# Two 64-row tiles for the remainder products of a column DFT, inside a stream of full-height matmuls

## The chip, the cores and the metric

The kernel runs on one core of one Trainium2 chip. The metric is the device time of one execution in microseconds, median of several.

## The reference, cut to what matters

```python
x  = A_x                                  # 1 x 2048 x 640, bf16
xn = layernorm(x)
X  = rfft2(xn) * (w_r + 1j * w_i)         # over 2048 rows and 640 columns
y  = irfft2(X)                            # bf16
h  = (xn @ w_gate) * (xn @ w_up)          # 640 -> 1536
return x + y + h @ w_down
```

The DFTs are done as matmuls. The step concerned is the DFT over the 640 columns. Symmetry folds 640 columns to 160, and 160 is 128 + 32: each of four groups g (even and odd output columns, cosine and sine) is one product over 128 rows plus a remainder over 32 rows. The four remainders together fill another 128 rows.

## The kernel before: the parts that matter

The remainder table puts group g on rows 32 g to 32 g + 31, and its columns in one of two halves of 320. So the first half (groups 0, 1) has only zeros below row 63, the second half (groups 2, 3) only zeros above row 64:

```python
fd = np.zeros((128, 4 * 160 + 640))
for g in range(4):
    fd[:, g * 160:(g + 1) * 160] = full[g][0:128]                                  # main
    fd[g * 32:(g + 1) * 32, 640 + g * 160:640 + (g + 1) * 160] = full[g][128:160]  # remainder
```

There are 16 D steps, t = 0 to 15. Each has two remainder products of 320 columns (line 887 of the kernel) and four main products of 160 columns (line 891), in two PSUM banks:

```python
def em_d(c, t=t):
    bk = bank_of(c.t)
    for h in range(2):
        c.e.matmul(ps[:, bk + h, 0:320], v_uq[:, 4, t, :], v_fd[:, 640 + 320 * h: 960 + 320 * h],
                   start=True, stop=False)                                  # L887
        for g in (2 * h, 2 * h + 1):
            o = (g % 2) * 160
            ins = c.e.matmul(ps[:, bk + h, o:o + 160], v_uq[:, g, t, :],
                             v_fd[:, g * 160:(g + 1) * 160],
                             start=False, stop=(g % 2 == 1))                # L891
    return ins
td = T("D_%d" % t, "pe", 2 * _d_mm(320) + 4 * _d_mm(160), em_d, ..., prio=pq, bank="pair", cls="a")
```

`T` records a task. A planner in the kernel's own Python orders all tasks on all engines by estimated durations, gives PSUM banks and sets the semaphore waits; the order is fixed when the program is built. Other lines that appear below: L844 gate and up products, L912 to L915 the next complex DFT step (C), L945 and L962 the inverse of it, L985 and L989 the inverse column DFT, L1030 the down product, L926 VectorE's filter multiply, L859 VectorE's product of gate and up, L677 the PSUM eviction (on ScalarE here).

Of the kernel before, what the change touches and what calls it, by code (L numbers as in the profile page):

```python
# [538 lines left out]
def _build(nc, A_x, A_w_r, A_w_i, B_w_gate, B_w_up, B_w_down, out, opts=None):  # L539
# [3 lines left out]
    with es:  # L543
# [56 lines left out]
        ps = es.enter_context(nc.psum_tensor("ps", [128, 8, 512], _F32))  # L600
# [3 lines left out]
        def V(name):  # L604
            off, sz = lay[name]
            return arena[:, off: off + sz]
# [5 lines left out]
        v_uq = V("U").rearrange("p (j t n) -> p j t n", j=5, t=16)  # L612
# [8 lines left out]
        v_fd = V("FD")  # L621
# [40 lines left out]
        def bank_of(t):  # L662
            return t.units[1]
# [207 lines left out]
        for t in range(16):  # L871
# [11 lines left out]
            def em_d(c, t=t):  # L883
                bk = bank_of(c.t)
                ins = None
                for h in range(2):
                    c.e.matmul(ps[:, bk + h, 0:320], v_uq[:, 4, t, :], v_fd[:, 640 + 320 * h: 960 + 320 * h],  # L887
                               start=True, stop=False)
                    for g in (2 * h, 2 * h + 1):
                        o = (g % 2) * 160  # L890
                        ins = c.e.matmul(ps[:, bk + h, o:o + 160], v_uq[:, g, t, :], v_fd[:, g * 160:(g + 1) * 160],  # L891
                                         start=False, stop=(g % 2 == 1))
                return ins
            td = T("D_%d" % t, "pe", 2 * _d_mm(320) + 4 * _d_mm(160), em_d, reads=[(b_u, None), (b_fd, None)],
                   prio=pq, bank="pair", cls="a")

# [231 lines left out]
```

## Time and profile before

| what | before | where it is read |
|---|---|---|
| device time | 223.86 us (223.76 to 224.03) | median of 4 runs |
| span of the profiled run | 221.8 us | head of the page |

That PE is the bound while the D steps run (85 to 119 us) is read from its waits, and the prediction below shows the lines. It misses one stall, which the table of PE's waits doesn't list because the record of the product ahead covers all but 10 ns of it. Two lines of the trace before show it:

```profile
88.80 0.30 PE L891 MATMUL ps<-arena 128*128 128x160 bf16 x2
89.11 0.99 PEld L844 LDWEIGHTS ps<-arena 128*128 128x128 bf16 x10 [0.21 <-DVE arena L926]
```

The second L891 starts at 88.87, and L844 would follow 69 ns later; it starts 243 ns later, so PE stands for 174 ns, for VectorE's filter multiply by the second line. It is the only stall of more than 20 ns in the D steps' stretch.

### The profile page before, as it was taken

What the parts mean: (1) busy time and instruction counts of PE and PEld (TensorE: products, weight loads), DVE (VectorE), ACT (ScalarE), POOL (GpSimd) and SP (SyncE); (2) the same over time, 40 slices, a digit from 0 to 9 for tenths busy, and PEclk for the clock granted to TensorE, in tenths of its full rate; (3) what the DMA queues carried; (4) which work ended last, traced back from release to release, by engine and by line L of the source; (5) the groups of instructions that cost most, each with busy time, mean ns of one, the idle gap of its engine ahead of it and who ended that gap; (6) DMA issues with size and microseconds to landing.
All of it is one profiled execution on the core that took longest, in us unless ns stands there. A gap on an engine that the chain in (4) does not pass through costs nothing.

```text
span 221.8 us, 5449 instructions
## 1 busy us (share of the span) xinstructions
PE 216.7 (98%) x2204; PEld 184.3 (83%) x2204; DVE 162.2 (73%) x481; ACT 112.0 (50%) x225; POOL 0.2 (0%) x4
## 2 busy tenths in 40 slices
PE   8999999999999999999999999999999999999995
PEld 8988999999999998888888898888867777777773
DVE  3779999999999994999999958998994222222321
ACT  2576888677777777777777566556520000000000
POOL 0000000000000000000000000000000000000000
DMA  7999995000000000232232029200002332323211
GB/s 197 303 345 392 413 371 92 3 4 0 0 3 0 4 0 3 46 65 62 63 67 55 7 85 317 77 0 3 0 15 78 102 98 79 106 86 106 77 44 44
DMA packets 22184, 21.16 MB, mean 95 GB/s; under 512 B 2192, under 2 KB 21008, under 8 KB 21904
## 3 DMA queue, kind: packets, MB, share of 16 engines
q1 hardware_dynamic: 20048, 19.74, 29.5%
q10 hardware_dynamic: 2112, 1.08, 1.9%
q8 instruction: 17, 0.28, 0.5%
q14 instruction: 7, 0.06, 0.1%
HBM read 18.19 MB, written 2.62 MB: 94 GB/s over the span
## 4 chain that ended last, share of the span: by engine, by line
PE 87%; DMA 4%; DVE 3%; SPq 3%; issue 1%; ACT 0%
PE ps L844 43%; PE ps L1030 23%; DMA arena<-in_A_x_dram 4%; PE ps L945 3%; SPq L671 3%; PE ps L807 2%; PE ps L891 2%; PE ps L887 2%; PE ps L1032 2%; PE ps L985 2%; PE ps L989 2%; PE ps L764 2%; PE ps L962 2%; PE ps L913 1%; PE ps L914 1%; PE ps L912 1%
## 5 line engine op out<-in xcount | busy, mean ns | idle before, releaser
L677 ACT ACTIVATE arena<-ps 128x512 bf16<-128x512 f32 (+5 forms) x214 | 109.3, 543 | 47.0 <-PE ps L844 37.7
L844 PE MATMUL ps<-arena 128*128 128x256 bf16 (+1 forms) x1200 | 115.5, 251 | 0.6 <-ACT arena L677 0.5
L844 PEld LDWEIGHTS ps<-arena 128*128 128x128 bf16 x1200 | 96.1, 98 | 9.1 <-issue 0.7
L1030 PE MATMUL ps<-arena 128*128 128x320 bf16 x384 | 56.6, 299 | 0.0
L1030 PEld LDWEIGHTS ps<-arena 128*128 128x128 bf16 x384 | 37.5, 98 | 14.5
L1039 DVE TENSOR_TENSOR arena<-ps,arena 128x320 bf16<-128x320 f32 x32 | 15.7, 491 | 37.2 <-PE ps L1032 37.2
L859 DVE TENSOR_TENSOR arena<-arena 128x256 bf16<-128x256 bf16 (+1 forms) x120 | 30.9, 258 | 11.9 <-ACT arena L677 9.6
L926 DVE TENSOR_TENSOR arena<-ps,arena 128x644 f32<-128x644 f32 x32 | 24.9, 819 | 1.3 <-PE ps L915 1.3
L723 DVE BATCH_NORM_STATS2 arena<-arena 128x6 f32<-128x320 bf16 x16 | 7.8, 485 | 4.5 <-DMA arena<-in_A_x_dram 4.5
L796 DVE TENSOR_TENSOR arena<-arena 128x256 bf16<-128x256 f32 (+1 forms) x32 | 10.2, 318 | 0.0
L797 DVE TENSOR_TENSOR arena<-arena 128x256 bf16<-128x256 f32 (+1 forms) x32 | 10.2, 317 | 0.0
L985 PE MATMUL ps<-arena 66*128 66x320 bf16 x32 | 9.3, 301 | 0.6 <-DVE arena L1013 0.6
L945 PE MATMUL ps<-arena 128*128 128x256 bf16 x64 | 9.6, 273 | 0.0
L1032 PE MATMUL ps<-arena 128*128 128x320 bf16 x32 | 9.6, 299 | 0.0
L989 PE MATMUL ps<-arena 128*128 128x160 bf16 x64 | 9.3, 231 | 0.0
L891 PE MATMUL ps<-arena 128*128 128x160 bf16 x64 | 9.1, 233 | 0.0
L887 PE MATMUL ps<-arena 128*128 128x320 bf16 x32 | 9.1, 299 | 0.0
L1004 DVE TENSOR_TENSOR arena<-ps,arena 128x320 f32<-128x320 f32 x16 | 7.8, 485 | 0.3
L935 DVE TENSOR_TENSOR arena<-arena 128x322 bf16<-128x322 f32 x16 | 7.8, 487 | 0.1
L1012 DVE TENSOR_TENSOR arena<-arena 128x320 bf16<-128x320 f32 x16 | 7.7, 484 | 0.1
L936 DVE TENSOR_TENSOR arena<-arena 128x322 bf16<-128x322 f32 x16 | 7.8, 486 | 0.0
L786 DVE TENSOR_TENSOR arena<-arena 128x320 f32<-128x320 bf16 x16 | 7.7, 483 | 0.0
(45 smaller groups left out, 157.9 us busy)
## 6 DMA issues: line engine op xcount, KB each, us to landing
arena<-in_A_x_dram SPq DMA_DIRECT2D x20, 160.0 KB, 2.3
out_dram<-arena SPq DMA_DIRECT2D x32, 80.0 KB, 1.6
arena<-c_ti SPq DMA_DIRECT2D x1, 2048.0 KB, 18.1
arena<-in_B_w_down_dram SPq DMA_DIRECT2D x1, 1920.0 KB, 9.2
arena<-c_tf SPq DMA_DIRECT2D x4, 384.0 KB, 11.6
arena<-in_A_w_r_dram SPq DMA_DIRECT2D x32, 40.1 KB, 2.2
arena<-in_A_w_i_dram SPq DMA_DIRECT2D x32, 40.1 KB, 2.3
arena<-in_B_w_gate_dram SPq DMA_DIRECT2D x4, 320.0 KB, 7.7
```

Source lines behind the costliest of these rows:

```text
L677: return c.e.activation(dst, src, _ACTF.Copy)
L844: ins = c.e.matmul(ps[:, bk, w * n:(w + 1) * n], v_gw[:, w, j, ft, :], v_xt[:, j, rows], start=(j == 0), stop=(j == 4))
L859: return c.e.tensor_tensor(v_ht[:, ft, rows], v_gbf[:, rr, 0:n], v_gbf[:, rr, n:2 * n], _OP.mult)
L887: c.e.matmul(ps[:, bk + h, 0:320], v_uq[:, 4, t, :], v_fd[:, 640 + 320 * h: 960 + 320 * h], start=True, stop=False)
L891: ins = c.e.matmul(ps[:, bk + h, o:o + 160], v_uq[:, g, t, :], v_fd[:, g * 160:(g + 1) * 160], start=False, stop=(g % 2 == 1))
L926: ins = c.e.tensor_tensor(v_p[:, r2, w, :, :].rearrange("p c (m e) -> p c e m", e=2), x4, wv, _OP.mult)
L945: ins = c.e.matmul(ps[:, bk, lt * 256:(lt + 1) * 256], v_y[:, r2, cc, lt:256:2], v_ti[:, t, cc, :], start=(cc == 0), stop=(cc == 1))
L985: c.e.matmul(ps[:, bk + h, 0:320], v_z2[0:66, 2, h, a, :], v_g[0:66, 640 + 320 * h: 960 + 320 * h], start=True, stop=False)
L989: ins = c.e.matmul(ps[:, bk + h, e * 160:(e + 1) * 160], v_z2[:, e, h, a, :], v_g[:, g * 160:(g + 1) * 160], start=False, stop=(e == 1))
L1030: c.e.matmul(ps[:, bk, 0:320], v_ht[:, ft, a * 128:(a + 1) * 128], v_wd[:, ft, sl3], start=(ft == 0), stop=False)
L1032: return c.e.matmul(ps[:, bk, 0:320], v_sm[:, 2, :], v_v[:, a, sl3], start=False, stop=True)
L1039: return c.e.tensor_tensor(v_out[:, a % 2, sl3], ps[:, bk, 0:320], v_xr[:, xs, sl3], _OP.add)
```

## The change

The intent is to run the two half-empty remainder products at the same time, each as a 64-row tile of the array, and so to save one streaming slot of 320 columns in every D step.

```diff
                 for h in range(2):
-                    c.e.matmul(ps[:, bk + h, 0:320], v_uq[:, 4, t, :], v_fd[:, 640 + 320 * h: 960 + 320 * h],
-                               start=True, stop=False)
-                    for g in (2 * h, 2 * h + 1):
-                        o = (g % 2) * 160
-                        ins = c.e.matmul(ps[:, bk + h, o:o + 160], v_uq[:, g, t, :], v_fd[:, g * 160:(g + 1) * 160],
-                                         start=False, stop=(g % 2 == 1))
+                    c.e.matmul(ps[:, bk + h, 0:320], v_uq[64 * h:64 * h + 64, 4, t, :],
+                               v_fd[64 * h:64 * h + 64, 640 + 320 * h:960 + 320 * h], start=True, stop=False)
+                for g in range(4):
+                    o = (g % 2) * 160
+                    ins = c.e.matmul(ps[:, bk + g // 2, o:o + 160], v_uq[:, g, t, :], v_fd[:, g * 160:(g + 1) * 160],
+                                     start=False, stop=(g % 2 == 1))
                 return ins
```

In the built program the remainder products are tiles of 64 x 128 at array rows 0 and 64, and all other products keep the mode of 128 x 128.

## The prediction

> **What bounds the kernel now.** I read the busy row first, then the chain that ended last, then the table of who waited for whom, and last the order of instructions in time over one turn of the loop that is changed. The page:
>
> ```profile
> PE 216.7 (98%) x2204; PEld 184.3 (83%) x2204; DVE 162.2 (73%) x481; ACT 112.0 (50%) x225; POOL 0.2 (0%) x4
> PE 87%; DMA 4%; DVE 3%; SPq 3%; issue 1%; ACT 0%
> L891 PE MATMUL ps<-arena 128*128 128x160 bf16 x64 | 9.1, 233 | 0.0
> L887 PE MATMUL ps<-arena 128*128 128x320 bf16 x32 | 9.1, 299 | 0.0
> ```
>
> The reader is to see three things. PE is busy for 216.7 of 221.8 us and is 87% of the chain that set the end. The two lines that the change touches, L887 (the remainder product, 32 times) and L891 (the four main products of each D step, 64 times), have no idle time before them. And the 299 ns of one L887 is not its price: 32 of them are "9.1 us busy" and 64 of L891 another 9.1, but matmuls overlap, so a price is the distance from one start to the next. That is in the matmuls of one D step in order of time (columns: start us, length us, engine, line, operation, count):
>
> ```profile
> 104.34 0.38 PE L962 MATMUL ps<-arena 128*66 128x256 bf16 x2
> 104.56 0.30 PE L887 MATMUL ps<-arena 128*128 128x320 bf16 x1
> 104.69 0.30 PE L891 MATMUL ps<-arena 128*128 128x160 bf16 x2
> 104.83 0.30 PE L887 MATMUL ps<-arena 128*128 128x320 bf16 x1
> 104.96 0.30 PE L891 MATMUL ps<-arena 128*128 128x160 bf16 x2
> 105.10 1.26 PE L844 MATMUL ps<-arena 128*128 128x256 bf16 x10
> ```
>
> A D step runs from 104.56 to 105.10: 0.54 us for 2 x 320 + 4 x 160 = 1280 columns, 0.422 ns a column, so 135 ns for one L887. The start-to-start distance (104.56 to 104.69) says the same. The other 299 - 135 = 164 ns of its record lie under the next matmul. There are 16 D steps, from 85.10 to about 119.4 us.
>
> Whether time taken from PE there reaches the end is a question of who waits. PE itself waited, in the whole execution:
>
> ```profile
> PE ps L704 <- DVE arena L711: 1.0, 1, 1.0
> PE ps L985 <- DVE arena L1013: 0.6, 2, 0.5
> PE ps L844 <- ACT arena L677: 0.5, 1, 0.5
> PE ps L764 <- DVE arena L729: 0.2, 1, 0.2
> ```
>
> None of these is inside the D stretch. The stretch itself, by engine (window, length, then busy us of PE, PEld, DVE, ACT, POOL, granted clock, DMA share, GB/s):
>
> ```profile
> 96.00:108.00 12.00, 12.00 (x113) 10.24 (x112) 11.40 (x23) 9.57 (x19) 0.00 (x0) 1.00 0.30 63
> 108.00:121.00 13.00, 13.00 (x122) 11.24 (x120) 11.89 (x23) 9.75 (x18) 0.00 (x0) 1.00 0.28 61
> ```
>
> PE has no gap at all, while VectorE has 1.7 us of idle in 25. One turn takes 2.84 us (D steps at 101.71, 104.56, 107.40). VectorE's order in time shows where its slack sits: once a turn it stands 0.27 us waiting for a ScalarE eviction.
>
> ```profile
> 104.18 0.29 DVE L859 TENSOR_TENSOR arena<-arena 128x256 bf16<-128x256 bf16 x1 [0.27 <-ACT arena L677]
> 107.02 0.29 DVE L859 TENSOR_TENSOR arena<-arena 128x256 bf16<-128x256 bf16 x1 [0.27 <-ACT arena L677]
> ```
>
> So PE bounds this stage with 0.27 us a turn to spare before VectorE would. The queue that loads the filter rows is third: four issues a turn, about 0.64 us each (pairs take 1.24 with a small gap), some 2.55 of 2.84 us.
>
> **What the Trainium skill says.** (1) "TensorE: Matmul & The Clock Gate", Part 3: operands on different row groups of the array run at once, starting about 4 ns apart, so a pack of two should cost little more than one matmul. Nothing in the trace before shows this; it has no row-tiled product. (2) "TensorEngine Tiling (Array Packing)", Key Properties: "Changing tiling mode (not just tile) drains the TensorE". It gives no time for the drain, and again the trace before has none: every matmul, the 66-row L985 too, is built for the full 128 x 128 array. (3) "TensorE: Matmul & The Clock Gate", Part 2, says that the fill and drain of successive matmuls overlap, that the next weights are loaded while a matmul streams, and splits the latency of an isolated matmul into about 60 cycles of issue, 128 of array drain and 31 of others. The trace agrees on the overlap: matmuls 135 ns apart with records of 299 ns, and weight loads of 98 ns that begin before the preceding products are done.
>
> **The change part by part.** Products, results and work of all other engines stay the same. The remainder table is block-shaped: the first half of its columns has non-zero rows 0 to 63 only, the second half 64 to 127 only, so half heights lose nothing and numbers stay as they were.
> - Removed: one streaming slot of 320 columns a D step, since the two remainder products now run side by side in two 64-row tiles and write two different banks. 16 x 135 ns = **2.16 us** if the overlap is complete. All lies on PE's gapless path.
> - Moved: the second remainder product goes ahead of all four main products. The order of instructions on PE is otherwise unchanged: the planner is still told two full durations, so no step moves against another, and the number of matmuls and weight loads stays 2204.
> - Added: two changes of tiling mode a D step, full to 64-row and back, as each pair stands between full-height products even where two D steps follow each other. I counted 32 in the built program; before there are none. Each may put a drain on the path that before was overlapped.
>
> With d the exposed time of one change, the net is 32 d - 2.16 us, and the change breaks even at **d = 68 ns**. What d may be, from numbers at hand:
> - nothing (mode travels with the instruction): 223.87 - 2.16 = 221.7 us.
> - array drain alone: 128 cycles at 2.4 GHz is 53 ns, an estimate from the page under (3): 32 x 0.053 = 1.7, net -0.5, so 223.4 us.
> - the tail of the record, 164 ns, exposed: 5.25 - 2.16 = +3.1, so 227.0 us.
> - that tail and then a weight load that could not be pulled ahead, 164 + 98 = 262 ns: 8.4 - 2.16 = +6.2, so 230.1 us.
>
> **The rivals.**
> A: overlap without a price, 221.7 us. For it: PE is the bound, the saving of 0.135 us a turn fits VectorE's 0.27 us and the load queue's 0.29 us, so it would travel to the end whole; after 121 us PE has only the 0.6 us wait at L985, which shifts along. Against: the page's sentence on the drain.
> B: the drains take back the gain or more, 223.4 to 230 us. For it: the sentence, 32 changes against 16 savings, and the fact that PE has no waits under which a drain could hide; every nanosecond is on the path. I hold this likelier than A, with d in the middle, because a drain has to wait for the last product's results and then cannot have its next weights early.
> C: VectorE or the load queue becomes the bound and caps the gain. For it: 95% and about 90% busy in the stretch. Against: the slacks just named are twice the saving. Worth at most some tenths: it would make 222.0 to 222.5 of A.
> D: the two tiles don't overlap, as both stream from the same buffer. Then nothing is saved and the drains come on top: 225.6 (d = 53) to 229 (d = 164). Little in the profile speaks for or against.
>
> **Range and chances.** I give A (with C) 0.25, a drain of 50 to 110 ns 0.3, 110 to 200 ns 0.25 and more 0.2. The middle of this lies at d near 90 ns: 32 x 0.09 - 2.16 = +0.7, so **224.5 us**. Eight in ten: 221.6 to 229.0. Faster by over 2% (below 219.4) would need twice the whole saving: 0.01. Slower by over 2% (above 228.35) needs d above 208 ns, or no overlap with d above 140: 0.18. Within 2%: 0.81.
>
> **What would show each step.** In the order of instructions in time, the two remainder products (now 64 rows) should start a few ns apart; 135 ns apart is D. From the last product before the pair to the pair, and from the pair to the first main product, the start distances should exceed those before by d each; none is A. A D step should take 0.54 - 0.135 + 2 d. VectorE's idle of 0.27 us a turn should fall to 0.13 (A), or grow by the added time (B). The table of waits should show no new wait of PE; one on VectorE or on a filter-row load is C. The prediction is wrong if d is far from 90 ns, or if a weight load for a half-height tile costs more than the 98 ns of today.

## More of the kernel before

One more view is needed to read the result, the weight loads (PEld) of one D step before (start us, length us, then engine, line, operation, count):

```profile
104.20 0.25 PEld L962 LDWEIGHTS ps<-arena 128*66 128x66 bf16 x2
104.45 0.10 PEld L887 LDWEIGHTS ps<-arena 128*128 128x128 bf16 x1
```

The product L887 itself starts at 104.56. Its weights begin to load at 104.45, 0.11 us earlier, while the second L962 product still streams.

## The result, and the profile after

| | before | after |
|---|---|---|
| device time, us | 223.86 (223.76 to 224.03), 4 runs | 225.01 (224.53 to 225.07), 4 runs |
| ratio | | 1.0046, 95% interval 1.0029 to 1.0063 |
| span of the profiled run, us | 221.8 | 223.1 |
| one turn with a D step, us | 2.84 | 2.92 |

A ratio is the mean time of one kernel's fast runs over that of the other's of the same rounds, so it is not quite the ratio of the medians. The change is 0.5% slower: within 2%, but clear of noise.

The page after, busy row and chain:

```profile
PE 217.9 (98%) x2204; PEld 181.6 (81%) x2204; DVE 162.3 (73%) x481; ACT 112.3 (50%) x225; POOL 0.2 (0%) x4
PE 87%; DMA 4%; DVE 3%; SPq 3%; issue 1%; ACT 0%
```

PE is still the bound, with the same number of instructions. The two groups of the D step after, by shape (busy us, mean ns, then idle before):

```profile
L891 PE MATMUL ps<-arena 128*128 128x160 bf16 x64 | 7.2, 235 | 0.0
L887 PE MATMUL ps<-arena 64*128 64x320 bf16 x32 | 5.0, 307 | 0.0
```

L887 fell from 9.1 to 5.0 us busy and L891 from 9.1 to 7.2, and neither has any idle before it: by the groups alone one would think that 6 us were won. The busy time of a group counts overlapping records once, so it falls when two products overlap, and the tail of a record (307 ns for 135 ns of streaming) covers the gap behind it. The gap shows only in the starts. The matmuls of one D step after:

```profile
105.11 0.38 PE L962 MATMUL ps<-arena 128*66 128x256 bf16 x2
105.42 0.31 PE L887 MATMUL ps<-arena 64*128 64x320 bf16 x2
105.66 0.45 PE L891 MATMUL ps<-arena 128*128 128x160 bf16 x4
105.95 1.25 PE L844 MATMUL ps<-arena 128*128 128x256 bf16 x10
```

From L962 to L844 it is now 0.84 us; before it was 0.76 (104.34 to 105.10). Both remainder products lie in one record pair of 0.31 us, so they do run together. But L962 to L887 grew from 0.22 to 0.31 us, and the pair is followed by its first main product only 0.24 us later, where one product of 320 columns takes 0.14. The weight loads of the same step:

```profile
104.97 0.25 PEld L962 LDWEIGHTS ps<-arena 128*66 128x66 bf16 x2
105.42 0.10 PEld L887 LDWEIGHTS ps<-arena 64*128 64x128 bf16 x2 [0.20 <-DVE arena L859]
105.66 0.25 PEld L891 LDWEIGHTS ps<-arena 128*128 128x128 bf16 x4
```

The weights no longer load early: load and product now start together, at 105.42 and again at 105.66. The bracket names a VectorE instruction as the releaser, but the table of waits of the matmuls has no such row (that of the weight loads has: L887 on L859, 1.6 us in 8 of 32 loads):

```profile
PE ps L704 <- DVE arena L711: 1.0, 1, 1.0
PE ps L844 <- ACT arena L677: 0.7, 1, 0.7
PE ps L985 <- DVE arena L1013: 0.7, 2, 0.5
```

The releaser is inferred from the last semaphore event; the start distances below show the same gap in every D step, also in those whose loads have no bracket. The run e1 below has the same order of instructions at full height, and no such gap. The time went into gaps that no view calls a wait. VectorE, in its order of time, only stands longer for the eviction that PE now feeds later:

```profile
104.95 0.29 DVE L859 TENSOR_TENSOR arena<-arena 128x256 bf16<-128x256 bf16 x1 [0.35 <-ACT arena L677]
107.87 0.29 DVE L859 TENSOR_TENSOR arena<-arena 128x256 bf16<-128x256 bf16 x1 [0.35 <-ACT arena L677]
```

It was 0.27 us, and the turn grew by the same 0.08 us.

The trace keeps starts to the nanosecond. Medians of the distance from one start to the next over all D steps, worked out from the matmul records:

```
from -> to                              before   after
L962 (256 columns) -> first L887          109     205     +96
first L887 -> second L887                   -       3.5
last L887 (320 columns) -> L891           136     239     +103
first L891 after the pair -> next L891     69      80     +11
other L891 -> L891                         69      69
```

Other products ahead of a pair give the same: L844 109 to 205.5, L915 (322 columns) 135.5 to 230.5, L891 69 to 165. The sum for one D step: 96 + 103 + 11 + 3.5 is 213.5 ns lost, 136 ns saved, net 77.5 ns; times 16 is 1.24 us, against 1.15 us between the medians.

The spans differ by 1.24 us too, but in part by chance. From the product ahead of the first D step to the one behind the last, the trace before takes 34.34 us and the trace after 35.42: 1.08 us more. The missing 0.15 us is the stall at 88.87, which shrank from 174 to 21 ns. Another 0.15 us of the spans' difference lies ahead of the first D step, where the wait of L844 for an eviction (0.5 us listed before, 0.7 after) differs as much without any tiles (0.8 us in e1).

### The profile page after: what moved, and what is told of

It reads as the page before. It is cut to its first block, busy times and chain, and to the rows that moved or that the text cites. A ratio compares the mean times of both kernels' runs of the same rounds, so it can differ in the third digit from the quotient of the medians.

```text
span 223.1 us, 5449 instructions
## 1 busy us (share of the span) xinstructions
PE 217.9 (98%) x2204; PEld 181.6 (81%) x2204; DVE 162.3 (73%) x481; ACT 112.3 (50%) x225; POOL 0.2 (0%) x4
## 3 DMA queue, kind: packets, MB, share of 16 engines
q10 hardware_dynamic: 2112, 1.08, 1.8%
## 4 chain that ended last, share of the span: by engine, by line
PE 87%; DMA 4%; DVE 3%; SPq 3%; issue 1%; ACT 0%
PE ps L844 43%; PE ps L1030 23%; DMA arena<-in_A_x_dram 4%; PE ps L945 3%; SPq L671 3%; PE ps L891 3%; PE ps L807 2%; PE ps L1032 2%; PE ps L887 2%; PE ps L985 2%; PE ps L989 2%; PE ps L764 2%; PE ps L962 2%; PE ps L913 1%; PE ps L914 1%; PE ps L915 1%
## 5 line engine op out<-in xcount | busy, mean ns | idle before, releaser
L677 ACT ACTIVATE arena<-ps 128x512 bf16<-128x512 f32 (+5 forms) x214 | 109.6, 543 | 47.8 <-PE ps L844 37.4
L844 PE MATMUL ps<-arena 128*128 128x256 bf16 (+1 forms) x1200 | 115.5, 251 | 0.7 <-ACT arena L677 0.7
L844 PEld LDWEIGHTS ps<-arena 128*128 128x128 bf16 x1200 | 96.0, 98 | 9.2 <-issue 0.9
L1030 PE MATMUL ps<-arena 128*128 128x320 bf16 x384 | 56.6, 299 | 0.0
L859 DVE TENSOR_TENSOR arena<-arena 128x256 bf16<-128x256 bf16 (+1 forms) x120 | 31.1, 259 | 12.4 <-ACT arena L677 10.0
L926 DVE TENSOR_TENSOR arena<-ps,arena 128x644 f32<-128x644 f32 x32 | 25.0, 823 | 1.5 <-PE ps L915 1.5
L985 PE MATMUL ps<-arena 66*128 66x320 bf16 x32 | 9.3, 301 | 0.7 <-DVE arena L1013 0.7
L945 PE MATMUL ps<-arena 128*128 128x256 bf16 x64 | 9.6, 273 | 0.0
L1032 PE MATMUL ps<-arena 128*128 128x320 bf16 x32 | 9.6, 300 | 0.0
L989 PE MATMUL ps<-arena 128*128 128x160 bf16 x64 | 9.3, 232 | 0.0
L1012 DVE TENSOR_TENSOR arena<-arena 128x320 bf16<-128x320 f32 x16 | 7.8, 487 | 0.1
L1013 DVE TENSOR_TENSOR arena<-arena 128x320 bf16<-128x320 f32 x16 | 7.8, 486 | 0.0
L786 DVE TENSOR_TENSOR arena<-arena 128x320 f32<-128x320 bf16 x16 | 7.8, 485 | 0.0
L785 DVE TENSOR_TENSOR arena<-arena 128x320 f32<-128x320 bf16 x16 | 7.8, 485 | 0.0
```

The costliest lines, as they stand in the source:

```text
L677: return c.e.activation(dst, src, _ACTF.Copy)
L844: ins = c.e.matmul(ps[:, bk, w * n:(w + 1) * n], v_gw[:, w, j, ft, :], v_xt[:, j, rows], start=(j == 0), stop=(j == 4))
L859: return c.e.tensor_tensor(v_ht[:, ft, rows], v_gbf[:, rr, 0:n], v_gbf[:, rr, n:2 * n], _OP.mult)
L926: ins = c.e.tensor_tensor(v_p[:, r2, w, :, :].rearrange("p c (m e) -> p c e m", e=2), x4, wv, _OP.mult)
L945: ins = c.e.matmul(ps[:, bk, lt * 256:(lt + 1) * 256], v_y[:, r2, cc, lt:256:2], v_ti[:, t, cc, :], start=(cc == 0), stop=(cc == 1))
L985: c.e.matmul(ps[:, bk + h, 0:320], v_z2[0:66, 2, h, a, :], v_g[0:66, 640 + 320 * h: 960 + 320 * h], start=True, stop=False)
```

## The experiments

My theory: each change between full-height and 64-row mode exposes about 0.1 us on PE, because the array must be empty before the next weights may load; the two tiles overlap fully; nothing else changed. Rivals: (R1) the order of the products costs time; (R2) the pair doesn't overlap fully and changes are cheap; (R3) any product of fewer rows than its neighbours stalls, whatever the mode; (R4) the gap is a late weight load and not the array. All experiments change only the D step; those of one table row are against the kernel before on the same chip.

| run | change of the D step | mode changes | overlapped slots | this, us | before, us | ratio (95%) |
|---|---|---|---|---|---|---|
| e1_full_reordered | order only | 0 | 0 | 223.92 | 223.89 | 0.9997 (0.9979 to 1.0015) |
| e2_one_half_tiled | one product tiled | 32 | 0 | 227.32 | 223.89 | 1.0151 (1.0133 to 1.0169) |
| e3_four_changes | both tiled, apart | 64 | 0 | 230.35 | 223.89 | 1.0288 (1.0269 to 1.0308) |
| e4_same_tile | both on one tile | 32 | 0 | 227.07 | 223.89 | 1.0142 (1.0115 to 1.017) |
| e5_66_rows | one product of 66 rows | 0 | 0 | 223.93 | 223.84 | 1.0000 (0.9986 to 1.0015) |
| v2_quad | two D steps in one, tiled | 16 | 16 | 224.31 | 223.84 | 1.0015 (1.0003 to 1.0028) |
| v3_quad_full | the same at full height | 0 | 0 | 224.82 | 223.84 | 1.0036 (1.0022 to 1.005) |
| v4_local_batches | tiled only where D steps adjoin | 6 | 7 | 224.29 | 223.97 | 1.0009 (0.9995 to 1.0022) |
| e6_96_columns | narrower tile weights | 32 | 16 | 225.23 | 223.97 | 1.0052 (1.0038 to 1.0065) |

The record marks all nine as correct. That includes e4 and e6, whose remainder products are wrong, so the mark says nothing about the remainder products of the others.

### e1_full_reordered: the order alone

```diff
-                    c.e.matmul(ps[:, bk + h, 0:320], v_uq[64 * h:64 * h + 64, 4, t, :],
-                               v_fd[64 * h:64 * h + 64, 640 + 320 * h:960 + 320 * h], start=True, stop=False)
+                    c.e.matmul(ps[:, bk + h, 0:320], v_uq[:, 4, t, :], v_fd[:, 640 + 320 * h:960 + 320 * h],
+                               start=True, stop=False)
```

> Both remainder products first, as in the changed kernel, but at full height: the order alone, no tiling. Drain theory (each change of tiling mode exposes about 100 ns on PE: (225.01 - 223.86 + 2.16) / 32 = 0.103 us): as the kernel before, 223.9 us, D step 0.54 us. Rival (the order itself, writing the second bank early, delays PE or an eviction): 224.5 to 225.

223.92 us against 223.89. The start distances are those of before (109, 136, 136, 69 ns). R1 falls.

### e2_one_half_tiled: two changes, no overlap

```diff
-                for h in range(2):
-                    c.e.matmul(ps[:, bk + h, 0:320], v_uq[64 * h:64 * h + 64, 4, t, :],
-                               v_fd[64 * h:64 * h + 64, 640 + 320 * h:960 + 320 * h], start=True, stop=False)
+                for h, r in ((0, slice(0, 64)), (1, slice(0, 128))):
+                    c.e.matmul(ps[:, bk + h, 0:320], v_uq[r, 4, t, :], v_fd[r, 640 + 320 * h:960 + 320 * h],
+                               start=True, stop=False)
```

> Only the first remainder product is a 64-row tile, the second stays at full height: two mode changes a D step as in the changed kernel, but no overlap to win. Drain theory: 223.9 + 32 x 0.10 = 227.1 us, with about 0.1 us more on each side of the tiled product. Rival (the changes are nearly free, and what was lost is that the pair did not overlap fully): 223.9 to 224.5.

227.32 us. 3.43 us for 32 changes is 0.107 us each. R2 falls: changes cost without any pair in sight. (By the stretch of the traces from the product ahead of the first D step to the one behind the last, with the stall of 175 ns that is gone here set right, it is 3.34 us against e1, 104 ns each.)

### e3_four_changes: twice as many changes

(shown against the changed kernel, cut)

```diff
-                for g in range(4):
-                    o = (g % 2) * 160
-                    ins = c.e.matmul(ps[:, bk + g // 2, ...
+                    for g in (2 * h, 2 * h + 1):        # back inside the loop over h, as before
+                        o = (g % 2) * 160
+                        ins = c.e.matmul(ps[:, bk + h, ...
```

> Both remainder products tiled but apart, each ahead of its own two main products as in the order of before: four mode changes a D step (64 in all), no overlap. Drain theory: 223.9 + 64 x 0.10 = 230.3 us, so twice the loss of the one-half kernel. Rival (nearly free changes): 223.9 to 224.5. If the cost depends on the matmul ahead of the change, the step from 32 to 64 differs from the step from 0 to 32.

230.35 us: 6.46 us for 64 changes is 0.101 us each, so the cost grows with the number of changes. (By the same stretch of the traces 6.69 us, again 104 to 105 ns each.) The second half of one D step and the first half of the next:

```profile
99.40 0.31 PE L887 MATMUL ps<-arena 64*128 64x320 bf16 x1
99.64 0.31 PE L891 MATMUL ps<-arena 128*128 128x160 bf16 x2
99.89 0.31 PE L887 MATMUL ps<-arena 64*128 64x320 bf16 x1
100.12 0.31 PE L891 MATMUL ps<-arena 128*128 128x160 bf16 x2
```

Every step down the page is 0.24 us, for 320 columns of one kind or 2 x 160 of the other: 0.14 us of streaming and 0.10 us of gap, whichever way the mode changes. The listed records of 0.31 us meet with no hole between them; only the starts tell.

### e4_same_tile: two changes, the pair one after the other

```diff
-                    c.e.matmul(ps[:, bk + h, 0:320], v_uq[64 * h:64 * h + 64, 4, t, :],
-                               v_fd[64 * h:64 * h + 64, 640 + 320 * h:960 + 320 * h], start=True, stop=False)
+                    c.e.matmul(ps[:, bk + h, 0:320], v_uq[0:64, 4, t, :],
+                               v_fd[0:64, 640 + 320 * h:960 + 320 * h], start=True, stop=False)
```

> Both remainder products on the same upper 64-row tile (wrong numbers on purpose): two changes a D step, no two tiles at once. If the pair of the changed kernel overlaps fully: 225.0 + 16 x 0.135 = 227.2 us and starts of the two 135 ns apart. If it did not overlap anyway: 225.0 us. If a weight load for the tile in use can't be pulled ahead, more than 227.2, with a gap between the two.

227.07 us, 2.06 us above the changed kernel, where full overlap is worth 16 x 0.136 = 2.18. (The changed kernel was timed in an earlier set of rounds; its ratio of 1.0046 against 1.0142 here says the same: 0.0096 x 223.9 = 2.1 us.) Between the traces, over the stretch of the D steps, it is 2.07 us. So the changed kernel's pair overlaps fully, and R2 falls a second time.

```profile
103.53 0.38 PE L962 MATMUL ps<-arena 128*66 128x256 bf16 x2
103.84 0.44 PE L887 MATMUL ps<-arena 64*128 64x320 bf16 x2
104.21 0.45 PE L891 MATMUL ps<-arena 128*128 128x160 bf16 x4
```

The pair is now 0.44 us long, not 0.31; the second starts 146 ns after the first by the records, 10 ns more than without a change before it. Behind the second product, L891 follows after 228 ns, 92 more than without a change; so of the 103 ns in the table above some 11 belong to the first product of the pair, and the gap on the way back to full height is 92 ns. The weights of the second load early, 10 ns after the first product started, although the same 64 rows are streaming. A stall comes with the change of mode, not with a second load onto a tile in use.

### e5_66_rows: a short product that keeps the mode

```diff
-                for h, r in ((0, slice(0, 64)), (1, slice(0, 128))):
+                for h, r in ((0, slice(0, 66)), (1, slice(0, 128))):
```

(against e2.) The two added rows of the table are zero.

> As the one-half kernel, but the first remainder product has 66 rows instead of 64, which is built for the full 128 x 128 array (its two more table rows are zero, so the result is right): a short product without a change of mode. Theory (it is the mode change that drains): 223.9 us, no gap beside it. Rival (any product of fewer rows than its neighbours can't have its weights early): about 227, as the one-half kernel.

223.93 us. The edit against e2 is two rows, and 3.4 us are gone:

```profile
104.52 0.38 PE L962 MATMUL ps<-arena 128*66 128x256 bf16 x2
104.74 0.44 PE L887 MATMUL ps<-arena 66*128 66x320 bf16 x2
105.02 0.44 PE L891 MATMUL ps<-arena 128*128 128x160 bf16 x4
```

L962 to L887 is 0.22 us again. R3 falls: what counts is the mode for which the product is built, 64 rows for 64 and the full array for 66. (Only these two heights were tried.)

### e6_96_columns: another weight load

```diff
-                    c.e.matmul(ps[:, bk + h, 0:320], v_uq[64 * h:64 * h + 64, 4, t, :], ..., start=True, stop=False)
+                    c.e.matmul(ps[0:96, bk + h, 0:320], v_uq[64 * h:64 * h + 64, 4, t, 0:96], ..., start=True, stop=True)
...
-                                     start=False, stop=(g % 2 == 1))
+                                     start=True, stop=True)
```

> The changed kernel with 96 instead of 128 columns of weights in the tiled products (their result is overwritten by the main products, wrong numbers on purpose), so that the weight load of the tile is another one. If the 96 ns ahead of the tiled pair are the array running empty: the same 96 ns, and 225.0 us. If they are a weight load that could not come early: they follow the length of the load (shorter with fewer columns, or longer if the 96-column load is the slower kind, as the 66-column load of 110 ns against 98 ns is), by 10 ns or more.

The load became longer with fewer columns: 116 ns, against 93 in the changed kernel.

```profile
L887 PEld LDWEIGHTS ps<-arena 64*96 64x96 bf16 x32 | 1.9, 116 | 3.1 <-DVE arena L859 1.6 <-issue 0.7 <-DVE arena L936 0.2
```

The distance ahead of the pair did not follow: 203 ns from L962 (205 with 128 columns), so the gap is still some 95 ns. The distance behind the pair did: 266 ns against 239, and the records of the pair grew from 307 to 333 ns. So the first gap does not depend on the load that comes after it; but a load that starts only with its product is itself partly exposed, and that part (27 ns more here) appears in the next distance. By the distances this should have cost 16 x 25 ns = 0.4 us. The stretch of the D steps is 0.36 us longer in this trace than in that of the changed kernel; the median moved by 0.22 us, from another set of rounds. So R4 is right only for a small part, by this reading the 10 or 11 ns by which the first product after a change is longer.

### v2_quad and v3_quad_full: half the changes for the same overlap

Two D steps become one task on four banks: the remainder products of both, then the eight main products. The planner was taught to hold two pairs of banks; v3 is the twin at full height with the same order of instructions.

```diff
+            if t % 2 == 0:
+                def em_d(c, t=t):
+                    bks = c.t.units[1]                      # two pairs of banks
+                    for j in range(2):
+                        for h in range(2):
+                            c.e.matmul(ps[:, bks[j] + h, 0:320], v_uq[64 * h:64 * h + 64, 4, t + j, :],   # v3: all 128 rows
+                                       v_fd[64 * h:64 * h + 64, 640 + 320 * h:960 + 320 * h], start=True, stop=False)
+                    for j in range(2):
+                        for g in range(4):
+                            ...                             # the main products of step t + j, as before
```

> Two D steps in one: four tiled remainder products (two pairs), then eight main products, on four banks held together; 16 mode changes instead of 32 for the same 16 overlapped slots. Theory: against its full-height twin in the same run -2.16 + 16 x 0.104 = -0.5 us, so about 223.4 us if the other order of steps costs nothing. Rival (the gain of overlap is lost on something else than the changes): no faster than the kernel before.

> The same two D steps in one and the same order of instructions, at full height: what batching alone does to the schedule, no mode change. Both theories: 223.9 us if VectorE and the banks keep up; anything above is the price of the batch.

The tiling did what the cost of a change says: v2 is 0.51 us faster than its twin (224.31 against 224.82), for an expected 0.5. But batching alone costs 0.98 us (224.82 against 223.84), which I had expected to be nothing. Three of the four waits of PE that the trace of the full-height twin lists:

```profile
PE ps L850 <- ACT arena L683: 1.0, 1, 1.0
PE ps L996 <- DVE arena L1024: 0.8, 2, 0.5
PE ps L850 <- DVE arena L937: 0.4, 1, 0.4
```

(L850, L683 and L937 are L844, L677 and L926 of the kernel before; six to eleven lines were added above them.) The wait of 0.4 us on the filter multiply is the stall at 88.87 of the kernel before, grown: L850 starts 625 ns after the last main product, against 243 before, 0.38 us more. Two further stalls, by the starts, are 0.10 us at L956 (L945 before) and 0.16 us more at L996 (L985 before). The first row says nothing of the batch: it lies near 20 us, before any D step, and varies from run to run. That makes some 0.64 us of the 0.98; the rest is not traced. So v2 loses to the kernel before by 0.15%.

### v4_local_batches: tiled only where the schedule already adjoins

Where D steps already follow each other on PE (steps 0 to 2, 3 and 4, and one more two), the first of the run draws all remainder products together and tiles them; single D steps stay at full height. The planner's order of tasks is untouched.

```diff
+                run = runs[t]                               # D steps that adjoin on PE
+                if t == run[0]:
+                    for u in run:
+                        bk = bank_of(tds_of[u])
+                        for h in range(2):
+                            r = slice(64 * h, 64 * h + 64) if len(run) > 1 else slice(0, 128)
+                            c.e.matmul(ps[:, bk + h, 0:320], v_uq[r, 4, u, :], ...)
```

> The kernel before with its schedule untouched, but where D steps already follow each other on PE (steps 0 to 2, 3 and 4, and one more two) their remainder products are drawn together and tiled: 7 overlapped slots for 6 mode changes. Theory: -7 x 0.136 + 6 x 0.105 = -0.32 us, 223.5 us. Rival (pulling remainder products ahead of earlier main products delays the evictions and PE waits, as in the batch of two everywhere): 223.9 or more. A gain this small is near what five rounds resolve.

224.29 against 223.97 us, interval 0.9995 to 1.0022: no gain, where 0.32 us was expected. The first run of three shows where it went:

```profile
85.33 0.58 PE L893 MATMUL ps<-arena 64*128 64x320 bf16 x6
85.84 1.00 PE L898 MATMUL ps<-arena 128*128 128x160 bf16 x12
87.17 0.30 PE L921 MATMUL ps<-arena 128*128 128x322 bf16 x1 [0.33 <-ACT arena L677]
```

(L893, L898 and L921 are the remainder, the main products and the first C product here.) The remainder products of steps 1 and 2 now run ahead of the main products of step 0, so step 0 is evicted later and C has to wait for the eviction: it starts 565 ns after the last main product, where 69 ns is the distance without a wait. That is 0.50 us lost, more than the 0.32 us won. Three shorter stalls (46 ns among the C products that follow, 40 and 117 ns around the third run) add 0.20 us. The rival was right.

No version tried beats the kernel before.

## Why the prediction was right

Predicted 224.5 us (221.6 to 229.0), within 2%; measured 225.01 us. By its own steps:

- **PE is the bound and every gain or loss there reaches the end.** Right but for one spot. No new wait of PE is listed, and of the 1.24 us that the start distances of the 16 D steps add up to, 1.08 us appear between the product ahead of the first D step and the one behind the last. "PE has no gap at all" was not quite so: the stall of 174 ns at 88.87 us, which the table of PE's waits doesn't list because the record of the product ahead covers all but 10 ns of it, took up the other 0.15 us.
- **Removed: 2.16 us if the overlap is complete.** Right. The pair starts 3.5 ns apart, and taking the overlap away (e4) costs 2.06 us.
- **The order costs nothing.** Right (e1).
- **Added: 32 changes, break-even at 68 ns.** Right in number and sign; e2 and e3 show that the cost belongs to the changes and grows with them.
- **The size of d.** Guessed near 90 ns, it measured (1.15 + 2.16) / 32 = 0.103 us in the changed kernel, 0.107 in e2 and 0.101 in e3. None of the four listed sizes hit: "array drain alone" (53 ns) was too small, the tail of the record (164 ns) too large, and the middle was a weighting, not a derivation. The 0.5 us by which the prediction fell short is this term: 32 x 13 ns = 0.4. The prediction's own chances, 0.25 at nothing and 0.3 for 50 to 110 ns, put the middle, if each is spread evenly, at d = 100 ns and so at 224.9 us; "near 90" was a slip. That the number came so near is in part luck, since nothing in the trace before gave d. ("TensorE: Matmul & The Clock Gate" of the Trainium skill, Part 2, from which the 53 ns are estimated, gives its split into 60, 128 and 31 cycles for the throttled clock; the estimate takes the 128 at the full one.)
- **That the drain then "cannot have its next weights early".** Half right. The loads do start late, together with their product, but only about 10 ns of a 93 to 98 ns load is exposed; the sum of 164 + 98 counted it whole.
- **Rivals.** A (no price) falls with e2; C (VectorE or the load queue caps the gain) was not put to the test, as there was no gain to cap; D (no overlap) falls with the starts 3.5 ns apart and with e4. B is what happened.

What stays open: whether the 96 ns are the array running empty or something else that belongs to the change of mode. They don't depend on the product ahead (four kinds, 95 to 97 ns over the distance of before) nor on the load behind (e6), which fits a fixed emptying time; no run looks inside it.

## What to carry to other kernels

Count mode changes before counting saved slots: here a pair of tiles amid full-height products paid two changes of about 0.105 us for one saved slot. At 0.425 ns a column (136 ns for 320), even a pair of 512 columns, the width of a PSUM bank in this kernel, would save an estimated 218 ns against 210 and just break even; two or more pairs must share one visit to pay, and gathering them must not delay what the other engines wait for. And when matmuls are packed closer, judge by the starts: the busy sums of the two changed lines fell by 6 us here while the kernel grew slower.

## What the Trainium skill lacked or had wrong

- "TensorEngine Tiling (Array Packing)", Key Properties, says that changing the tiling mode drains the engine, without a cost, and gives no break-even for a pair of tiles. Here one change cost 0.101 to 0.107 us of PE time by the medians, 104 to 105 ns by the starts: 96 ns more between the product ahead and the pair, for four kinds of product ahead, or 92 ns on the way back, plus 10 or 11 ns in the first product behind. A pair of 320 columns saved 136 ns and paid about 210.
- "TensorE: Matmul & The Clock Gate", Part 3, "What overlaps and what doesn't", has weight loads overlap running matmuls only on other row groups. The trace differs: full-height loads started 0.11 us ahead of their product while full-height products streamed, and two products on the same 64-row tile started 146 ns apart, where full-height ones start 136 ns apart, with no drain between. It sides with the page's Part 2, which the prediction cites: the next weights are loaded while a matmul streams.
- The same page's formula for a weight load (columns over 1.2 GHz: 80 ns for 96 columns, 107 ns for 128) goes the wrong way here: 64 x 96 took 116 ns and 64 x 128 took 93 ns. The page's table on fast weight load, which it ties to 128 weights, does fit this order.
- In no page: that such a drain is listed nowhere as a wait. The pages warn only in general that matmul busy time is a bad measure and that the ends of matmuls are estimated. Here the 0.20 us gap of the weight loads was put down to a VectorE instruction, and the two changed matmul groups showed 0.0 idle.
